# Leftover rows spread over 16 DMA engines, one first-layer pair in four through the score banks, and an order from a forward-backward scheduler, in a fused sparse attention and rational MLP kernel

## The chip, the cores and the metric

The kernel runs on one core of one Trainium2 chip. The metric is the device time of one execution in microseconds. Before the change three runs took 400.84, 405.41 and 404.82 us, median 404.82 us. One further execution was profiled: 402.03 us, with a span of 400.0 us between the first and the last thing that the profile shows.

The engines are TensorE (PE in the profile; PEld is its weight load), VectorE (DVE), ScalarE (ACT), GpSimd (POOL) and SyncE (SP). In this kernel POOL and SP do next to nothing but issue DMAs, each in the order of its own list.

## The reference

The work is an attention with two kinds of sparse mask, whose output is reshaped to 4,608 tokens of 512 features and put through two dense layers with a rational activation between them.

```python
B, H, S, D = 8, 8, 576, 64          # stride = 32
scores = (1 / sqrt(D)) * q @ k.transpose(0, 1, 3, 2)
rel = pos[:, None] - pos[None, :]
mask_local   = (rel >= 0) & (rel < stride)                      # heads 0 to 3
mask_strided = (rel >= 0) & (pos % stride equal for query, key)  # heads 4 to 7
scores = where(mask, scores, -1e9)
attn = softmax(scores)
x = (attn @ v).transpose(0, 2, 1, 3).reshape(4608, 512)
h = x @ w_in                        # 512 x 2048
P = a[0] + a[1] * h + a[2] * h**2 + a[3] * h**3
Q = 1 + |b[0]| * |h| + |b[1]| * h**2
out = (P / (Q + 1e-6)) @ w_out      # 2048 x 512
```

Inputs and outputs are float32; the kernel computes in bfloat16 with float32 sums.

## The kernel before

**Batches and chunks.** The eight batches of the attention go one after another (batch 0 to 7). The first 512 of a batch's 576 positions give four tiles of 128 tokens, which make up one chunk of 512 tokens for the dense layers (chunk 0 to 7). The 64 leftover positions of all batches make up chunk 8, the last.

**Attention of one batch.** `loads` and its helpers fetch the batch. `load_qk` brings the 512 main rows of q and k in two parts: part 0 is heads 4 to 7 (strided mask), part 1 is heads 0 to 3 (local mask), into `qn` and `kn`; part 2 brings the leftover rows into `qm` and `km`. `load_v` brings v into `VL` (local heads), `VT` (strided heads) and `VW` (leftover rows of the strided heads). All of these are issued by POOL, since they also turn float32 into bfloat16; the q, k and v of batch 0 alone come as float32 through SP and are turned by DVE, ACT and POOL. `scores` then has these steps:

- T: SP issues four DMA transposes of part 0 into `sT` (batch 0 does it on PE). `sT` has one buffer, so batch b+1's transposes wait for the last matmul of batch b that reads it.
- R2, R3: PE rearranges part 1 of k and q through PSUM into `kL` and `qL`.
- S and L: PE computes the strided and the local scores in PSUM on top of a mask that is added by matmuls; ACT takes the exponential into `ES` and `EL`.
- TL and X: SP issues two DMA transposes of the leftover rows into `LT`; PE computes the leftover rows' scores; ACT takes the exponential into `EX` and `EW`. This is the step that frees `sT`.

`attend` multiplies by v (five tiles, four main and one leftover), DVE divides by the row sums into `XR`, and SP issues a DMA transpose of each tile into `XT` (leftover tile: `XW`). Batches 0 and 1 transpose their main tiles on PE.

**Dense layers.** `dense1` is the first layer of a chunk: 16 blocks of 128 hidden features, computed two by two ("a pair", 8 matmuls of 128x512) into one of four PSUM tiles; ACT copies a pair to `HB`. Then comes the rational function: DVE takes |h| (L991 on uint16 views), b1|h|+b0 (L1003), times |h| (L1006); ACT makes 1/Q by Ln and Exp (L1015, L1018); DVE evaluates P by Horner (L1029, L1032, L1034, L1036, L1039) and multiplies with 1/Q (L1042). Chunks 2 to 7 do the DVE steps on all 16 blocks at once (8,192 elements a partition), the others in smaller groups. `dense2` is the second layer (64 matmuls of 128x512 a chunk, in groups of 8), and ACT copies its result to `OS`, from which SP writes to HBM.

**PSUM.** Four tiles of two banks each: S (scores), A (attention output), H and O. First-layer pairs alternate between H and O for chunks 0 to 2 and use H alone from chunk 3 on; the second layer uses O, and A and S for the last chunk.

**What sets the order.** Nothing in the program text does. Every operation is recorded with its engine, its dependencies, an estimated cost and a key. `Program.schedule` runs a list scheduler over them: whenever an engine is free, it takes the ready operation with the lowest key. The keys come from the table `KT` (about one number for each kind of operation and batch or chunk). The result is one fixed list for each engine, and an engine works through its list strictly in turn, waiting on semaphores at its head. Matmuls of all kinds are recorded through two helper lines, so the profile knows them as L634 (and L637 for PE transposes); they are told apart by their tiles.

Of the kernel before, what the change touches and what calls it, by code (L numbers as in the profile page):

```python
# [15 lines left out]
def _bf16_bits(x):  # L16
# [26 lines left out]
}  # L43

# [58 lines left out]
class Program:  # L103
# [32 lines left out]
    def schedule(self):  # L136
        import heapq
        for i, op in enumerate(self.ops):
            op.idx = i
            op.nwait = 0  # L140
            op.ready = 0.0
# [18 lines left out]
        while left:  # L160
# [15 lines left out]
            t, e = best  # L176
# [133 lines left out]
def bass_strided_sparse_attn__then__act_rational_pade_kernel(nc, q, k, v, moe_w_in, moe_w_out, moe_a, moe_b, out):  # L310
# [8 lines left out]
    CH = 512  # L319
# [3 lines left out]
    HL, NHO, DA, TB, NF0 = 4, 3, 0, 1, 70  # L323
# [72 lines left out]
    mz = np.where((hh_[:, None] == hh_[None, :]) & (dz >= 0) & (dz % 8 == 0), 0.0, NEG)  # L396
    rx = np.zeros((64, 192))
# [91 lines left out]
    def load_qk(b, key, part, x):  # L489
# [8 lines left out]
        else:  # L498
            add("POOL", (lambda e: e.dma_start(
                sml[i][64:128, 0:256], src[b, 4:8, 512:576, :].rearrange("h (p g) d -> h p (g d)", g=4))),  # L500
                [n_free[x][2][i], ini[id(sml[i])], hw0], 0.7, key, g, 0.25)
            for hh in range(2):
                add("POOL", (lambda e, hh=hh: e.dma_start(
# [91 lines left out]
    def loads(b):  # L595
        if b == 0:
            loads0()
            for x in (1, 0):
                load_qk(0, -955 - x, 2, x)
# [577 lines left out]
```

## Time and profile before

| | |
|---|---|
| three runs | 400.84, 405.41, 404.82 us |
| median | 404.82 us |
| profiled execution | 402.03 us |
| its span | 400.0 us |
| mean granted TensorE clock | 0.92 |
| busy: PE, DVE, ACT, POOL | 329.1, 322.8, 267.6, 171.3 us |
| DMA packets, bytes | 148,631, 41.87 MB |

Busy time of an engine is a mean over stages that are limited by different things, so the share alone decides nothing; the table by stretch and the chain of waits do. In the rows below a line number is that of the kernel before; `psS<-LT` reads "written to PSUM tile S, read from LT". In a row of the chain of waits the two numbers are start and length in us.

### The profile page before, as it was taken

To read this page: it belongs to the slowest core of one execution; us is meant where nothing else is said; L and a number is where in the kernel's file an instruction comes from. 1 tells how busy PE (TensorE), PEld (TensorE's weight loads), DVE (VectorE), ACT (ScalarE), POOL (GpSimd) and SP (SyncE) were. 2 spreads that over 40 slices of the span, in tenths; PEclk is the share of its full clock that TensorE was granted. 3 is DMA by queue.
4 is the path that set the end of the run, shared out by engine and by line. 5 is a ranking of instruction groups with operands and counts; after the bars stand their busy time and mean duration, and the time that the engine had idled before them with its cause. 6 is when DMAs were issued, how large, how long until landed. Compare 5 with 4: busy or idle time off the path is not lost.

```text
span 400.0 us, 9314 instructions
## 1 busy us (share of the span) xinstructions
PE 329.1 (82%) x4150; PEld 164.6 (41%) x4150; DVE 322.8 (81%) x276; ACT 267.6 (67%) x228; POOL 171.3 (43%) x203
## 2 busy tenths in 40 slices
PE   6686258457999769989999998999999999869930
PEld 6543225133544324444444544444444455534400
DVE  3436875965999997468998999999999899999930
ACT  2516366657498838856996799898379579686320
POOL 0999488225695489369657904900000000000000
PEclk9959759958999969999999999999999999998965
DMA  7999999999999998899999588743022222202202
GB/s 243 199 99 170 150 148 75 144 190 137 108 130 131 148 132 81 112 164 158 129 160 111 55 117 85 110 81 77 12 51 54 52 54 52 52 2 52 52 23 82
DMA packets 148631, 41.87 MB, mean 105 GB/s; under 512 B 121328, under 2 KB 143536, under 8 KB 148592
## 3 DMA queue, kind: packets, MB, share of 16 engines
q0 software_dynamic: 97376, 16.94, 52.7%
q1 hardware_dynamic: 51216, 24.34, 32.9%
q8 instruction: 32, 0.52, 0.6%
q14 instruction: 7, 0.06, 0.1%
HBM read 36.90 MB, written 9.44 MB: 116 GB/s over the span
## 4 chain that ended last, share of the span: by engine, by line
PE 36%; DVE 28%; DMA 16%; POOL 5%; SPq 5%; ACT 5%; issue 2%
PE psO L634 17%; PE psH L634 14%; DMA LT<-qm 5%; DVE UU L1006 4%; DVE T L1032 4%; DVE T L1042 3%; DVE T L1036 3%; DMA sT<-qn 3%; DVE UU L1003 3%; DVE T L991 3%; DVE T L1029 2%; PE psA L634 2%; SPq L691 2%; PE psS L634 2%; DMA XT<-XR 2%; DVE XR L885 2%
## 5 line engine op out<-in xcount | busy, mean ns | idle before, releaser
L634 PE MATMUL psO<-Wout,T 128*128 128x512 bf16 x512 | 120.8, 385 | 3.1 <-ACT OS L1106 3.1
L634 PE MATMUL psH<-XT,Win 128*128 128x512 bf16 x416 | 104.1, 394 | 9.9 <-DMA XT<-XR 6.1
L977 ACT ACTIVATE HB<-psH 128x1024 bf16<-128x1024 f32 x60 | 61.3, 1022 | 39.5 <-PE psH L634 39.2
L1015 ACT ACTIVATE UU<-UU,cst 128x2048 bf16<-128x2048 bf16 (+1 forms) x38 | 72.5, 1908 | 15.7 <-DVE UU L1006 15.6
L634 PEld LDWEIGHTS psO<-Wout,T 128*128 128x128 bf16 x512 | 48.6, 99 | 60.9 <-ACT OS L1106 4.1
L1018 ACT ACTIVATE UU<-UU 128x2048 bf16<-128x2048 bf16 (+1 forms) x38 | 69.2, 1822 | 0.6
L634 PEld LDWEIGHTS psH<-XT,Win 128*128 128x128 bf16 x416 | 39.7, 100 | 60.8 <-issue 7.0
L1042 DVE TENSOR_TENSOR T<-T,UU 128x4096 bf16<-128x4096 bf16 (+2 forms) x23 | 41.8, 1825 | 10.2 <-ACT UU L1018 9.8
L1006 DVE TENSOR_TENSOR UU<-UU,T 128x4096 bf16<-128x4096 bf16 (+2 forms) x23 | 41.6, 1825 | 0.5
L1032 DVE TENSOR_TENSOR T<-T,HB 128x8192 bf16<-128x8192 bf16 (+3 forms) x17 | 41.1, 2417 | 0.5
L1036 DVE TENSOR_TENSOR T<-T,HB 128x8192 bf16<-128x8192 bf16 (+3 forms) x17 | 41.0, 2414 | 0.4
L536 POOL DMA_DIRECT2D VT<-in_v_dram x48 | 37.9, 818 | 0.0
L524 POOL DMA_DIRECT2D VL<-in_v_dram x24 | 22.1, 937 | 27.2 <-PE psA L634 27.2
L991 DVE TENSOR_SCALAR T<-HB 128x8192 uint16<-128x8192 uint16 (+3 forms) x17 | 23.4, 1378 | 12.4 <-ACT HB L977 12.4
L1003 DVE TENSOR_SCALAR UU<-T,coef 128x4096 bf16<-128x4096 bf16 (+2 forms) x23 | 25.5, 1121 | 0.6
L634 PE MATMUL psO<-XT,Win 128*128 128x512 bf16 x96 | 24.4, 399 | 0.0
L1029 DVE TENSOR_SCALAR T<-HB,coef 128x8192 bf16<-128x8192 bf16 (+3 forms) x17 | 24.0, 1413 | 0.4
L885 DVE TENSOR_TENSOR XR<-psA,RC 128x512 bf16<-128x512 f32 (+1 forms) x35 | 22.1, 630 | 2.8 <-DMA XT<-XR 1.6
L1039 DVE TENSOR_SCALAR T<-T,coef 128x8192 bf16<-128x8192 bf16 (+3 forms) x17 | 23.6, 1386 | 0.4
L1034 DVE TENSOR_SCALAR T<-T,coef 128x8192 bf16<-128x8192 bf16 (+3 forms) x17 | 23.5, 1380 | 0.4
L1106 ACT ACTIVATE OS<-psO 128x1024 f32<-128x1024 f32 x16 | 16.4, 1022 | 9.2 <-PE psO L634 9.1
L544 POOL DMA_DIRECT2D VW<-in_v_dram x28 | 22.5, 813 | 0.0
(151 smaller groups left out, 383.6 us busy)
## 6 DMA issues: line engine op xcount, KB each, us to landing
out_dram<-OS SPq DMA_DIRECT2D x72, 128.0 KB
kn<-in_k_dram POOLq DMA_DIRECT2D x14, 256.0 KB, 5.9
qn<-in_q_dram POOLq DMA_DIRECT2D x14, 256.0 KB, 6.9
Win<-in_moe_w_in_dram POOLq DMA_DIRECT2D x4, 512.0 KB, 9.6
Wout<-in_moe_w_out_dram POOLq DMA_DIRECT2D x1, 2048.0 KB, 18.8
VL<-in_v_dram POOLq DMA_DIRECT2D x24, 72.0 KB, 4.4
VT<-in_v_dram POOLq DMA_DIRECT2D x48, 32.0 KB, 3.3
HB<-in_k_dram SPq DMA_DIRECT2D x2, 512.0 KB, 5.1
```

Of the source, the lines that this page charges most:

```text
L536: add("POOL", (lambda e, h=h, c=c: e.dma_start(VT[i][64 * c:64 * c + 64, h, :, 0:64], v[b, 4 + h, 0:512, :].rearrange("(x c g) d -> c x g ...
L634: return lambda e: e.matmul(out_ap, l, r, start=start, stop=stop, skip_group_check=True)
L977: o2 = add("ACT", (lambda a, hb=hb, ps=ps, f=f: a.activation(hb[:, f:f + 2, :], ps[:, :, :], AF.Copy)), [o1, old], ca(1024), key.of("HB"))
L991: d1 = add("DVE", (lambda d, hb=hb, t3=t3, g_=g_: d.tensor_scalar(t3.bitcast(dt.uint16)[:, g_, :], hb.bitcast(dt.uint16)[:, g_, :], 0x7FFF ...
L1003: d2 = add("DVE", (lambda d, u=u, t3=t3, sl=sl, HG=HG: d.tensor_scalar(u[:, 0:HG, :], t3[:, sl, :], b1_ap, b0_ap, op0=Alu.mult, op1=Alu.add)),
L1006: d3 = add("DVE", (lambda d, u=u, t3=t3, sl=sl, HG=HG: d.tensor_tensor(u[:, 0:HG, :], u[:, 0:HG, :], t3[:, sl, :], op=Alu.mult)), [d2], ct ...
L1015: ln = add("ACT", (lambda a, u=u, zl=zl: a.activation(u[:, zl, :], u[:, zl, :], AF.Ln, bias=cst[:, 0:1], scale=1.0)), [d3, cons], 0.28 + w ...
L1018: ex.append(add("ACT", (lambda a, u=u, zl=zl: a.activation(u[:, zl, :], u[:, zl, :], AF.Exp, scale=-1.0)), [ln], 0.21 + w * 0.000833, kz + ...
L1029: d4.append(add("DVE", (lambda d, hb=hb, t3=t3, h0=h0, h1=f0 + gn: d.tensor_scalar(t3[:, h0:h1, :], hb[:, h0:h1, :], a_ap[3], a_ap[2], op0 ...
L1032: d5 = add("DVE", (lambda d, hb=hb, t3=t3, g_=g_: d.tensor_tensor(t3[:, g_, :], t3[:, g_, :], hb[:, g_, :], op=Alu.mult)), [d4], ctt(n), k ...
L1036: d7 = add("DVE", (lambda d, hb=hb, t3=t3, g_=g_: d.tensor_tensor(t3[:, g_, :], t3[:, g_, :], hb[:, g_, :], op=Alu.mult)), [d6], ctt(n), k ...
L1042: d9 = add("DVE", (lambda d, t3=t3, u=u, sl=sl, HG=HG: d.tensor_tensor(t3[:, sl, :], t3[:, sl, :], u[:, 0:HG, :], op=Alu.mult)), [d8, ex], ...
```

## The change

1. **Leftover rows.** The DRAM side of the leftover loads is written with the 16 groups of rows as the outer dimension instead of the heads: `qm` and `km` rows of the strided heads, and `VW`. For the local heads two DMAs, of two heads each, become four, of one head each. The leftover rows of the strided heads thus stand in `qm`/`km` in another order, and the mask columns and the slices that read `LT` are permuted to match. 32 more DMAs are issued by POOL over the run.
2. **PSUM tiles.** From chunk 3 on, every fourth first-layer pair goes to S instead of H (`PM1 = "HHHS"`). A tile is chosen by name tables (`PM1`, `PM2`, `PAV`, `PSC`).
3. **A piece of the polynomial.** `DA` goes from 0 to 1: in chunks 2 to 7 the first Horner step a3·h+a2 is done by ACT for 8 of the 16 blocks (one instruction on 4,096 elements), by DVE for the other 8.
4. **Order.** `KT` has other numbers, and above all every operation's key is replaced by its place in a fixed list `PRIORITY` of 1,230 entries, which a forward-backward scheduler has made. `loads` no longer has a special order for batch 1, all four loads of `Win` are recorded together, and the load of `Wout` is recorded behind the loads of batch 2. In `dense2` the groups of one PSUM tile now depend on each other, so that no list can turn them round.

```diff
+PRIORITY = [
+    6, 49, 160, 166, 162, 191, 51, 9, 8, 76, 108, 20, 21, 107, 186, 179, 188, 18, 22, 73, 33, 34, 68, 48,
...
+    1222, 1228, 1226, 1225, 1229
+]
...
         for i, op in enumerate(self.ops):
             op.idx = i
+            if PRIORITY:
+                op.key = PRIORITY[i]
...
-    HL, NHO, DA, TB, NF0 = 4, 3, 0, 1, 70
+    HL, DA, TB, NF0 = 4, 1, 1, 70
+    PM1, PM2, PAV, PSC = "HHHS", "O", "A", "S"
...
+    mz = mz[:, 16 * (ar % 4) + ar // 4]
...
             add("POOL", (lambda e: e.dma_start(
-                sml[i][64:128, 0:256], src[b, 4:8, 512:576, :].rearrange("h (p g) d -> h p (g d)", g=4))),
+                sml[i][64:128, 0:256], src[b, 4:8, 512:576, :].rearrange("h (p g) d -> p h (g d)", g=4))),
...
-            for hh in range(2):
-                add("POOL", (lambda e, hh=hh: e.dma_start(
-                    sml[i][0:32, :].rearrange("x (g y d) -> x y g d", g=4, y=2)[:, hh],
-                    src[b, hh:4:2, 512:576, :].rearrange("a (p g) d -> a p g d", g=4))),
-                    [n_free[x][2][i], ini[id(sml[i])], hw0], 0.7, key + 0.01, g, 0.15)
+            for h in range(4):
+                add("POOL", (lambda e, h=h: e.dma_start(
+                    sml[i][16 * (h // 2):16 * (h // 2) + 16, :].rearrange("x (g y d) -> x y g d", g=4, y=2)[:, h % 2],
+                    src[b, h, 512:576, :].rearrange("(p g) d -> p g d", g=4))),
+                    [n_free[x][2][i], ini[id(sml[i])], hw0], 0.65, key + 0.01, g, 0.15)
...
-                        v[b, 4:8, 512:576, :].rearrange("h (i g) d -> g h i d", g=4)[2 * gp + j])),
+                        v[b, 4:8, 512:576, :].rearrange("h (i g) d -> g i h d", g=4)[2 * gp + j])),
...
-                                             LT[64 * j:64 * j + 64, 0, gh, 64 + 16 * h:80 + 16 * h], False, False))
+                                             LT[64 * j:64 * j + 64, 0, gh, 64 + h:128:4], False, False))
...
-                pn = "HO"[npair[0] % 2] if c < NHO else "H"
+                pm = "HO" if c < 3 else PM1
+                pn = pm[npair[0] % len(pm)]
...
-                    last = add("PE", makers, [[res[kk][2] for kk in range(q0, q0 + 4)], g2.ops, p_free[pn]],
+                    last = add("PE", makers, [[res[kk][2] for kk in range(q0, q0 + 4)], g2.ops, p_free[pn], last],
```

The change moves nearly every instruction. Three places show what the next part speaks of; an `x2` at a row's end means two such instructions in a row.

The first is POOL's list around the load of `Wout` (the second layer's weights). Before, from the leftover rows of batch 2 on (L499, L503, `VW`) to the main rows of batch 3 (`kn`, `qn`):

```order
L499 DMA km<-in_k_dram 64x1x256
L499 DMA qm<-in_q_dram 64x1x256
L503 DMA km<-in_k_dram 32x4x64 x2
L503 DMA qm<-in_q_dram 32x4x64 x2
L536 DMA VT<-in_v_dram 64x4x64
L544 DMA VW<-in_v_dram 64x1x64 x4
L486 DMA Wout<-in_moe_w_out_dram 128x16x512
L495 DMA kn<-in_k_dram 128x4x256
L495 DMA qn<-in_q_dram 128x4x256
```

After, from the same leftover rows on (L575, L579 are the lines that were L499, L503; L571 was L495, L562 was L486, L620 was L544):

```order
L579 DMA qm<-in_q_dram 16x4x64 x2
L575 DMA km<-in_k_dram 64x1x256
L571 DMA qn<-in_q_dram 128x4x256
L579 DMA qm<-in_q_dram 16x4x64
L579 DMA km<-in_k_dram 16x4x64
L571 DMA kn<-in_k_dram 128x4x256
L562 DMA Wout<-in_moe_w_out_dram 128x16x512
L620 DMA VW<-in_v_dram 64x1x64
L571 DMA kn<-in_k_dram 128x4x256
```

`Wout` has moved behind the first q and k loads of batch 3, which can only be issued once batch 2's transposes into `sT` have read `qn` and `kn`. Two of the leftover loads of batch 2 now stand behind such a q load too.

The second place is PE's list from the scores of batch 2 to its leftover scores (the rows with `LT`). Before, from the mask and the strided scores (`psS<-sT`) on:

```order
L634 MATMUL psS<-IDN,MK 64x512 x4
L634 MATMUL psS<-sT 64x64 x32
L634 MATMUL psS<-IDN,MK 64x512 x4
L634 MATMUL psS<-qL,kL 64x32 x64
L634 MATMUL psA<-VL,EL 32x65 x16
L634 MATMUL psA<-VT,ES 32x65 x16
L634 MATMUL psH<-XT,Win 128x512 x8
L634 MATMUL psS<-MK 64x192 x4
L634 MATMUL psS<-IDN,MK 64x64 x4
L634 MATMUL psS<-LT,kL 64x32 x8
```

After, the end of the same stretch; five pairs (`XT,Win`) and all four main tiles of the attention (`VL,EL` with `VT,ES`) stand between the local scores and the leftover scores, of which these are the last three pairs and two tiles (L700 was L634):

```order
L700 MATMUL psH<-XT,Win 128x512 x8
L700 MATMUL psA<-VL,EL 32x65 x16
L700 MATMUL psA<-VT,ES 32x65 x16
L700 MATMUL psO<-XT,Win 128x512 x8
L700 MATMUL psA<-VL,EL 32x65 x16
L700 MATMUL psA<-VT,ES 32x65 x16
L700 MATMUL psH<-XT,Win 128x512 x8
L700 MATMUL psS<-MK 64x192 x4
L700 MATMUL psS<-IDN,MK 64x64 x4
L700 MATMUL psS<-LT,kL 64x32 x8
```

So the leftover scores, which wait for the transposes into `LT`, stand several microseconds of matmuls later in the list, behind work that does not need them.

The third place is PE's list where the first pairs of chunk 3 begin (`psH<-XT,Win`), among the second layer of chunk 0 (`psO<-Wout,T`) and the scores of batch 4. Before:

```order
L634 MATMUL psO<-Wout,T 128x512 x8
L637 MATMUL psS<-IDN,qn 64x128 x16
L634 MATMUL psH<-XT,Win 128x512 x8
L634 MATMUL psO<-Wout,T 128x512 x8
L634 MATMUL psS<-IDN,MK 64x512 x4
L634 MATMUL psS<-sT 64x64 x32
L634 MATMUL psH<-XT,Win 128x512 x8
L634 MATMUL psO<-Wout,T 128x512 x8
```

After:

```order
L700 MATMUL psO<-Wout,T 128x512 x16
L700 MATMUL psH<-XT,Win 128x512 x8
L700 MATMUL psS<-MK 64x192 x4
L700 MATMUL psS<-IDN,MK 64x64 x4
L700 MATMUL psS<-LT,kL 64x32 x8
L700 MATMUL psS<-LT,sT 64x16 x32
L700 MATMUL psS<-LT 64x64 x4
L700 MATMUL psO<-Wout,T 128x512 x8
L700 MATMUL psH<-XT,Win 128x512 x8
L700 MATMUL psS<-XT,Win 128x512 x8
```

Before, four groups of chunk 0's second layer stand ahead of chunk 3's first pair; now all eight do. From the first to the last pair of chunk 3 seven second-layer groups stood in between, now four. The last row is a pair in PSUM tile S.

At the start SP's list has changed as well: the float32 q of heads 0 to 3 goes first, then v, then the constants and the rest of q and k. POOL's first loads (`Win`) wait for the q load of heads 0 to 3, which was the fourth of SP's loads and is now the first. At the end the last four pairs of chunk 8 have four second-layer groups between them each.

More of the change, by code (lines that the diff above doesn't have):

```diff
@@ L591, in loads0 @@
         t3_free[1] = [evl, v_ev[1, 0]]
-        load_win(0, -990)
-        load_win(1, -989)
+        for z in range(NW1):
+            load_win(z, Key("LW", z))
     def loads(b):
@@ L681, in scores @@
                 key = Key("X", b, n)
-            pn = sets.get(name, "S")
+            pn = sets.get(name, "S") if first else PSC[nsc[0] % len(PSC)]
+            nsc[0] += name not in ("T", "TL")
             ps = PS[pn]
@@ L1074, in dense2 @@
         tail = c == NCH - 1
-        used = ["A", "S"] if tail else ["O", "O"]
+        used = ["A", "S"] if tail else [PM2[(2 * c + z) % len(PM2)] for z in range(2)]
         if tail:
@@ L1083, in dense2 @@
                             makers.append(mm(ps[:, e_, :], gl(res[kk], 2 * i2 + e_), Wout[:, kk, :], kk == 0, kk == NF - 1))
[L1084 removed]
+                    o = add("PE", makers, [[res[kk][2] for kk in range(q0, q0 + 2)], g2.ops, p_free[used[i2]], done[-2:]],
+                            4 * 0.216, base + q0 + 0.1 * i2)
                     done.append(o)
@@ L1089, in dense2 @@
             if not tail:
+                last = []
                 for q0 in range(0, NF, 4):
```

35 lines of the change are left out of this document (12 added, 23 removed), and 104 rows, old and new, of tables (KT, PRIORITY).

## The prediction

> **What bounds the kernel now.** I read the page first, then a table of busy time by stretch, then the chain of work that ended last, then the waits. The page's head and three of its rows of 40 slices of 10 us:
>
> ```profile
> span 400.0 us, 9314 instructions
> PE 329.1 (82%) x4150; PEld 164.6 (41%) x4150; DVE 322.8 (81%) x276; ACT 267.6 (67%) x228; POOL 171.3 (43%) x203
> PE   6686258457999769989999998999999999869930
> DVE  3436875965999997468998999999999899999930
> PEclk9959759958999969999999999999999999998965
> ```
>
> PE and DVE are both four fifths busy, and each has its gaps mostly in the first 18 slices. There the granted clock falls to 0.5 as well. The table by stretch puts numbers to that (columns: length, busy us of PE, PEld, DVE, ACT, POOL, clock, DMA share, GB/s):
>
> ```profile
> 75.00:100.00 25.00, 12.92 (x276) 6.28 (x276) 16.13 (x17) 16.72 (x15) 8.19 (x10) 0.73 1.37 166
> 100.00:135.00 35.00, 33.75 (x558) 16.77 (x559) 34.24 (x35) 27.59 (x25) 25.66 (x29) 1.00 1.22 125
> 135.00:150.00 15.00, 8.86 (x78) 3.60 (x77) 14.79 (x9) 6.88 (x7) 9.52 (x10) 0.77 1.28 142
> 150.00:180.00 30.00, 28.56 (x428) 13.69 (x430) 18.20 (x16) 22.77 (x22) 20.25 (x25) 1.00 1.13 119
> 180.00:250.00 70.00, 67.21 (x1107) 33.04 (x1104) 65.52 (x44) 58.46 (x54) 43.44 (x49) 1.00 1.03 116
> 250.00:310.00 60.00, 59.97 (x434) 27.00 (x433) 59.12 (x33) 48.33 (x35) 9.15 (x10) 1.00 0.35 64
> 310.00:340.00 30.00, 30.00 (x156) 15.12 (x155) 28.17 (x12) 23.11 (x18) 0.00 (x0) 1.00 0.23 53
> 340.00:385.00 45.00, 38.57 (x184) 17.96 (x181) 41.53 (x40) 27.13 (x20) 0.00 (x0) 0.95 0.15 35
> ```
>
> Between 75 and 100 us PE and DVE both idle and the clock is 0.73: 8.9 us of DVE are lost. Between 135 and 180 PE idles first, at clock 0.77, and DVE afterwards: 12.0 us of DVE are lost, 11.8 of them after 150. From 180 to 340 PE misses 2.8 us of 160 and DVE 7.2; ACT misses 30.1. After 340 it is DVE. The chain says why (start, length, what):
>
> ```profile
> 19.10 5.51 DMA qm<-in_q_dram
> 77.57 14.23 DMA LT<-qm
> 135.15 8.12 DMA XT<-XR
> 143.31 3.59 PE psH L634 x8
> 308.68 1.73 PE psH L634 x8
> 312.17 1.02 ACT OS L1106
> 315.03 2.29 DVE T L1042
> 381.96 0.70 DVE T L1042
> ```
>
> The early losses are DMAs: the leftover rows at 19, the transposes of batch 2's leftover rows, 14.2 us on their way, and the transposes of chunk 3's input, 8.1 us. Through the middle the chain is PE at 1.73 us a group of 8 matmuls, from 313 on ACT and DVE.
>
> **The leftover loads.** What they cost, from the DMA view (size, median us to landing) and the groups (count, busy, mean ns):
>
> ```profile
> qm<-in_q_dram POOLq DMA_DIRECT2D x16, 16.0 KB, 4.8
> km<-in_k_dram POOLq DMA_DIRECT2D x16, 16.0 KB, 5.5
> VT<-in_v_dram POOLq DMA_DIRECT2D x48, 32.0 KB, 3.3
> L503 POOL DMA_DIRECT2D km<-in_k_dram x16 | 18.6, 1167 | 0.1
> L499 POOL DMA_DIRECT2D qm<-in_q_dram x8 | 5.2, 653 | 0.0
> ```
>
> The nearest row for a small load with 64 partitions outside on both sides is `VT`, twice as large and 2.2 us faster than `km`. So batch 0's leftover rows, which are on the chain, gain up to 2.2 us. Against that POOL issues four DMAs of 64 rows for two of 128: a row of that size takes 0.65 us (L499), so 4 x 0.65 - 2 x 1.17 = 0.3 us more for `km`, and about as much for `qm`, under 1 us for a batch. I take -1 us, ends -2.2 and +1. The Trainium skill ("DMA: Bandwidth & Descriptors", rules for kernel authors) says that the outermost dimension caps the engines a DMA uses, which gives the same sign. Another rule on that page speaks against this edit: join small transfers, since under 64 KB a DMA is mostly overhead. By it the two extra DMAs would cost and nothing would land sooner: +1 instead of -1. I keep the `VT` row as the nearer evidence; no run here separates the two yet. The permuted mask and the strided slices of `LT` change no count; I put them at nothing.
>
> **`Wout` and batch 2.** Two rows of the lists of POOL and SP, one of the DMA view, and four of the waits (total, times, longest):
>
> ```profile
> 71.04 1.18 POOL L486 DMA_DIRECT2D Wout<-in_moe_w_out_dram  x1
> 70.39 2.92 SPq L691 DMA_TRANSPOSE sT<-qn  x2
> Wout<-in_moe_w_out_dram POOLq DMA_DIRECT2D x1, 2048.0 KB, 18.8
> PE psS L634 <- DMA sT<-qn: 7.3, 1, 7.3
> PE psH L634 <- ACT HB L977: 4.0, 7, 1.2
> PE psH L634 <- DMA XT<-XR: 6.1, 1, 6.1
> ACT HB L977 <- PE psH L634: 39.2, 28, 7.3
> ```
>
> `Wout` is issued while batch 2's transposes into `sT` are under way, and takes 18.8 us. PE then waits 7.3 us for those transposes, and later for `LT`. In the new list `Wout` stands behind q and k loads that need these transposes finished, so it can't slow them. It now meets the transposes into `LT` and `XT` of batch 2, but PE's list has five pairs (5 x 1.73 = 8.7 us) and four attention tiles before the leftover scores where it had one of each. What is late next is therefore `XT` of batch 2, with those five pairs as its cover too. I take -7.3 us for this stretch; it cannot give more than the 8.9 us that DVE loses there, nor less than 0. One new wait: POOL's q load of batch 3 waits for `sT`, and behind it are the last two leftover loads of batch 2, then SP's `LT` transposes, then the leftover scores. If the pairs don't cover that, part of the 7.3 comes back.
>
> **Chunk 3.** PE's first pair of chunk 3 waits for `XT` until 143.3 and then runs at half pace: 3.59 us against 1.73. In the new list eight second-layer groups stand ahead of it instead of four: 4 x 1.73 = 6.9 us later, about the 6.1 us that PE waits there for `XT`, so the pair starts where it did, without the wait and warm (-1.9). Four instead of seven groups stand between its pairs: -3 x 1.73 = -5.2 us to the last one, which lets DVE's 16-block steps begin. Together about -7; since the first layer of other chunks moves as well, I take -6, ends 0 and -11.8 (all that DVE loses after 150).
>
> **The Horner step on ACT.** By shape:
>
> ```profile
> L1029 DVE TENSOR_SCALAR T<-HB,coef 128x8192 bf16<-128x8192 bf16 x6 | 14.5, 2422 | 0.2
> L1029 DVE TENSOR_SCALAR T<-HB,coef 128x4096 bf16<-128x4096 bf16 x3 | 4.0, 1342 | 0.1
> L1015 ACT ACTIVATE UU<-UU,cst 128x2048 bf16<-128x2048 bf16 x34 | 67.9, 1997 | 7.7 <-DVE UU L1006 7.7
> ```
>
> DVE saves 6 x (2.42 - 1.34) = 6.5 us. Only where DVE is the later engine does that shorten anything: for certain in chunk 7 (1.1 us), at most everywhere. I take half, 3.5 us. ACT has no such instruction now; L1015 takes 2.0 us for 2,048 elements, so 4,096 take between 2.0 and 4.0, and I take 3.9, near the upper end: 23.4 us more on ACT. Its cover is ACT's idle time, 30.1 us from 180 to 340, where five of the six fall (19.5 us): 0 for now, but ACT would be 93% busy there.
>
> **Pairs in S; the rest of the order.** PE waits 4.0 us for the copy out of H in the whole run: the fourth pair in S can save at most that and must share S with the scores. I take 0, ends 0 and -4. The dependencies in `dense2` are between PE's own instructions and cost nothing. At the start q of heads 0 to 3 goes first, and `Win` follows its landing:
>
> ```profile
> 10.16 1.69 POOL L481 DMA_DIRECT2D Win<-in_moe_w_in_dram  x2 [9.71 <-DMA HB<-in_q_dram]
> 7.14 6.43 DMA T<-in_v_dram
> 13.60 1.91 ACT L644 ACTIVATE VL<-T 32x2048 bf16<-32x2048 f32 x1 [0.89 <-DMA T<-in_v_dram]
> HB<-in_k_dram SPq DMA_DIRECT2D x2, 512.0 KB, 5.1
> ```
>
> Of the four loads of q and k the last lands at 10.2 us, each some 5 to 6 us after its issue, so three of them share the last 4 us or so. With `Win` beside them instead of after them these may take twice as long: +4. v would land sooner, and ACT's turning of v (1.9 us), which now stands between its landing and the exponentials, would be done before the scores come: -2. I take 0.
>
> **Sum.** -1 - 7.3 - 6 - 3.5 = -17.8 on the profiled 402.0: 384.2 us. That execution lies 2.8 us under the median of the three runs, but above their lowest, so I put 1.4 on top: 386 us.
>
> **Rivals.** (a) *The collision only moves.* `Wout` keeps DMA busy for 18.8 us wherever it is; it now meets the transposes of `LT`, `XT` and then `sT` of batch 3, and chunk 3 starts no earlier because more stands before it. For it: DMA share above 1 in every stretch shown up to 250 us. Against it: PE's list has work ahead of the late steps. Only -3.5 and -1 are left: 402.0 - 4.5 + 1.4 = 399 us. (b) *ACT becomes the bound, and it is slower.* ACT works its list in turn; a 3.9 us instruction stands ahead of the copies that free H, and PE and DVE wait for these. ACT waits 39.2 us for PE in the whole run, so its idle time is not free to be filled at will. If the 30.1 us of idle time between 180 and 340 stay and five such instructions (19.5 us) come on top, with -7.3 and -1 from the early part: 402.0 + 19.5 - 8.3 + 1.4 = 415 us. It decides from the point where ACT's idle time in that stretch does not fall below 30 - 19.5 = 11 us. (c) *All bounds on the good side:* -2.2 - 8.9 - 11.8 - 6.5 - 4 - 2 = -35.4, so 368 us.
>
> **How the numbers follow.** The forecast has 0.57, (a) 0.20, (b) 0.11, (c) 0.12. The range reaches from 370 us, 2 us short of all bounds at once, to 403 us, which is (a) with the +4 of the start, and leaves (b) out. A difference of 2% is what runs of this kernel tell from none (they spread over 1.1%): faster than 396.7 us by the forecast and (c) together, 0.69; within 2% for (a), 0.20; slower than 412.9 us for (b), 0.11.
>
> **What would show it.** Right: PE's wait for `sT<-qn` near 80 us gone, no 14 us step for `LT` in the chain, DVE busy for more than 16.1 of the 25 us from 75 to 100; chunk 3's first pair at 1.73 us; landing of `km` near 3.3 us; DVE about 316 us busy in total, ACT about 291; no new wait of PE for HB beyond some 4 us. Wrong: an `XT` or `LT` transpose of over 10 us with PE idle behind it anywhere before 180 us, or ACT over 95% busy from 180 to 340 with PE waiting on its copies.

## The result, and the profile after

The changed kernel takes 392.5 us (median of four runs, 391.4 to 393.6); the kernel before takes 404.5 us (median of four, 400.8 to 405.4). The ratio is 0.972, with a 95% interval of 0.9654 to 0.9786: faster by 2.8%. I had forecast 386 us, with a range of 370 to 403 us.

| | before | after |
|---|---|---|
| median of the runs | 404.5 us | 392.5 us |
| profiled execution, its span | 402.0, 400.0 us | 393.6, 391.5 us |
| busy: PE, DVE | 329.1, 322.8 us | 321.6, 315.3 us |
| busy: ACT, POOL | 267.6, 171.3 us | 286.8, 169.5 us |
| DMA packets | 148,631 | 111,255 |

The page of the changed kernel, three of its rows of 40 slices (9.8 us each):

```profile
span 391.5 us, 9332 instructions
PE 321.6 (82%) x4119; PEld 164.5 (42%) x4150; DVE 315.3 (81%) x276; ACT 286.8 (73%) x234; POOL 169.5 (43%) x235
PE   0858976973799839989999999989999999997930
DVE  2433995975879895687999999999999999999930
PEclk9966996995799987998999999999999999999995
```

The holes of the first 18 slices are still there. The table by stretch, in the columns of the prediction (length, busy us of PE, PEld, DVE, ACT, POOL, clock, DMA share, GB/s):

```profile
75.00:100.00 25.00, 13.25 (x235) 6.88 (x233) 18.20 (x22) 17.71 (x16) 10.61 (x16) 0.80 1.32 165
100.00:135.00 35.00, 32.67 (x515) 16.31 (x520) 29.33 (x29) 28.20 (x25) 25.13 (x33) 0.95 0.96 104
135.00:150.00 15.00, 8.75 (x134) 3.84 (x132) 14.76 (x10) 5.99 (x5) 13.53 (x19) 0.82 1.72 168
150.00:180.00 30.00, 27.62 (x444) 14.02 (x448) 17.80 (x16) 25.14 (x22) 15.24 (x24) 0.92 1.13 138
180.00:250.00 70.00, 67.59 (x896) 32.90 (x905) 68.86 (x47) 63.74 (x52) 41.65 (x50) 1.00 0.82 110
250.00:310.00 60.00, 58.27 (x538) 27.12 (x542) 58.75 (x33) 56.25 (x41) 7.48 (x12) 1.00 0.33 58
310.00:340.00 30.00, 28.94 (x157) 15.31 (x158) 29.65 (x14) 29.46 (x20) 0.00 (x0) 1.00 0.23 53
```

Compare with the rows before. From 75 to 100 us DVE does 18.2 us of work instead of 16.1. From 100 to 180 it does 61.9 us instead of 67.2. Up to 180 us it is idle for 3.9 us more than before (its work before 75 us is 43.3 instead of 43.8 us), so nothing is won by then. From 180 to 340 it is idle for 2.7 of 160 us instead of 7.2. And DVE has 7.5 us less to do in the whole run (315.3 against 322.8), while the span is 8.5 us shorter: DVE's idle time in all hardly moved (76.2 us against 77.2). ACT is busy for 149.5 of the 160 us from 180 to 340, 93%.

The chain of waits shows where the early time went (start, length, what):

```profile
10.75 11.28 DMA coef<-in_moe_a_dram
34.31 3.59 PE psO L700 x8
79.97 12.59 DMA XT<-XR
93.37 7.06 DMA XT<-XR
100.48 3.37 PE psO L700 x8
136.88 9.72 DMA XT<-XR
146.65 3.61 PE psH L700 x8
```

The three `PE ... x8` rows are the first pairs of chunks 0, 2 and 3. Ahead of the second stand two `XT` transposes of batch 2 that take 12.6 and 7.1 us; ahead of the third, one of 9.7 us. Six rows of the waits (total, times, longest) say who stands still:

```profile
PE psO L700 <- DMA XT<-XR: 5.3, 1, 5.3
DVE XR L953 <- DMA XT<-XR: 6.3, 1, 6.3
PE psH L700 <- DMA XT<-XR: 6.8, 2, 6.1
POOL qm L579 <- DMA LT<-km: 12.1, 1, 12.1
ACT HB L1045 <- PE psH L700: 13.3, 18, 1.8
PE psH L700 <- ACT HB L1045: 1.1, 3, 0.5
```

PE's wait for `sT` of batch 2 (7.3 us before) is gone, but PE now waits 5.3 us for chunk 2's `XT` (the first row). Between the two slow transposes stands DVE: it waits 6.3 us for the first one, which reads `XR`, before it can write the last main tile of batch 2 into the same buffer, so that the second one is issued only at 93.4 us. The 6.1 us wait for chunk 3's `XT` is what it was, and POOL waits 12.1 us for a transpose into `LT`. ACT's waits for PE's pairs in H fell from 39.2 to 13.3 us; part of that idle time now holds the six new instructions.

At the start the two kernels differ like this: DVE's instructions around the copy into `sT` after the change, then PE's first pair before and after it.

```profile
20.42 0.69 DVE L711 CAST VT<-T 128x1024 bf16<-128x1024 f32 x1 [6.39 <-DMA T<-in_v_dram]
22.05 0.16 DVE L510 SCALAR_TENSOR_TENSOR coef<-coef 128x2 f32<-128x2 f32 x1 [0.94 <-DMA coef<-in_moe_a_dram]
22.13 1.22 DVE L711 COPY sT<-psS 128x2048 bf16<-128x2048 bf16 x1
```

```profile
25.47 3.39 PE L634 MATMUL psH<-XT,Win 128*128 128x512 bf16 x8 [0.69 <-ACT XT L644]
```

```profile
34.31 3.59 PE L700 MATMUL psO<-XT,Win 128*128 128x512 bf16 x8 [0.52 <-DVE XT L711]
```

The new list has two small operations that wait for late DMAs, on v and on the coefficients, ahead of the copy into `sT`, for which PE waits 4.4 us. And SP issues the second half of q at 6.8 us instead of 2.8, behind the loads of v and the identity, so that ACT turns it at 15.95 us instead of 9.87. The first pair comes 8.8 us later.

So two questions are open. Which part of the change made the 12 us? And what were the early stalls worth, since some moved, some stayed, and one was added?

### The profile page after: what moved, and what is told of

Same layout as the page of the kernel before. It is cut to its first block, busy times and chain, and to the rows that moved or that the text cites. A ratio compares the mean times of both kernels' runs of the same rounds, so it can differ in the third digit from the quotient of the medians.

```text
span 391.5 us, 9332 instructions
## 1 busy us (share of the span) xinstructions
PE 321.6 (82%) x4119; PEld 164.5 (42%) x4150; DVE 315.3 (81%) x276; ACT 286.8 (73%) x234; POOL 169.5 (43%) x235
## 2 busy tenths in 40 slices
DMA packets 111255, 41.72 MB, mean 107 GB/s; under 512 B 83952, under 2 KB 106160, under 8 KB 111216
## 4 chain that ended last, share of the span: by engine, by line
DVE 37%; PE 25%; DMA 19%; POOL 5%; SPq 5%; issue 4%; ACT 2%; POOLq 0%; DVEq 0%
PE psO L700 9%; DMA XT<-XR 9%; PE psH L700 8%; DVE T L1104 6%; DVE UU L1074 5%; DVE T L1100 5%; DVE T L1110 5%; PE psS L700 3%; PE psA L700 3%; DVE T L1107 3%; DVE T L1102 3%; DMA coef<-in_moe_a_dram 3%; DVE UU L1071 3%; POOL VT L612 3%; POOL VL L600 2%
## 5 line engine op out<-in xcount | busy, mean ns | idle before, releaser
L700 PE MATMUL psO<-Wout,T 128*128 128x512 bf16 x482 | 111.4, 379 | 4.4 <-issue 2.4
L700 PE MATMUL psH<-XT,Win 128*128 128x512 bf16 x336 | 82.8, 389 | 7.9 <-DMA XT<-XR 6.8
L700 PEld LDWEIGHTS psO<-Wout,T 128*128 128x128 bf16 x512 | 48.4, 98 | 57.3 <-ACT OS L1176 1.4
L1045 ACT ACTIVATE HB<-psH 128x1024 bf16<-128x1024 f32 x48 | 49.1, 1024 | 13.4 <-PE psH L700 13.3
L700 PEld LDWEIGHTS psH<-XT,Win 128*128 128x128 bf16 x336 | 31.5, 98 | 47.5 <-DMA XT<-XR 7.4
L600 POOL DMA_DIRECT2D VL<-in_v_dram x24 | 25.6, 1074 | 28.4 <-PE psA L700 28.1
L612 POOL DMA_DIRECT2D VT<-in_v_dram x48 | 35.9, 778 | 2.4 <-PE psA L700 1.8
L700 PE MATMUL psO<-XT,Win 128*128 128x512 bf16 x96 | 25.9, 417 | 5.8 <-DMA XT<-XR 5.3
L579 POOL DMA_DIRECT2D qm<-in_q_dram x32 | 20.4, 643 | 12.1 <-DMA LT<-km 12.1
L1093 ACT ACTIVATE T<-HB,coef 128x4096 bf16<-128x4096 bf16 x6 | 22.8, 3799 | 0.9 <-DVE UU L1074 0.9
L951 DVE RECIPROCAL RC<-psA 128x8 f32<-128x8 f32 (+1 forms) x35 | 6.9, 197 | 19.0 <-PE psA L700 18.8
## 6 DMA issues: line engine op xcount, KB each, us to landing
Wout<-in_moe_w_out_dram POOLq DMA_DIRECT2D x1, 2048.0 KB, 18.9
```

The source lines that it names most:

```text
L612: add("POOL", (lambda e, h=h, c=c: e.dma_start(VT[i][64 * c:64 * c + 64, h, :, 0:64], v[b, 4 + h, 0:512, :].rearrange("(x c g) d -> c x g ...
L700: return lambda e: e.matmul(out_ap, l, r, start=start, stop=stop, skip_group_check=True)
L1045: o2 = add("ACT", (lambda a, hb=hb, ps=ps, f=f: a.activation(hb[:, f:f + 2, :], ps[:, :, :], AF.Copy)), [o1, old], ca(1024), key.of("HB"))
```

## Experiments: the parts against the order

My theory after the two traces: DVE's smaller work is the gain, the early stalls cancel out. The rivals: the loads, or the order itself. Each kernel was timed beside the kernel before on the same chip (405.05 us there, median of 17, for the first four). A ratio is that of a kernel's time to the time of the kernel before, with its 95% interval in brackets.

**The table of order numbers taken away.**

```
 PRIORITY = [
-    6, 49, 160, 166, 162, 191, 51, 9, 8, ...
 ]
```

> The changed kernel, but its table of order numbers is empty, so that the list scheduler goes by the formula keys that stand beside it; loads, the Horner step on ScalarE and the fourth pair in S stay. DVE was busy 7.5 us less after the change (315.3 against 322.8) while the span fell by 8.5 us. If the smaller work of DVE is the whole gain, this kernel has that work too and takes 392 to 396 us. If the order carries the gain, or is needed to make room for ScalarE's larger share, it takes 401 us or more, with the difference in idle time of DVE.

Measured: 418.4 us (413.8 to 420.2), ratio 1.032 (1.0267 to 1.0375). All the other parts are in it, DVE's smaller work too (314.9 us), and it is slower than the kernel before. So the smaller work is not the whole gain. Two waits show where the formula keys lose: in the execution profiled (420.2 us) DVE waits 19.2 us for ACT's half of the Horner step, and PE 20.8 us for transposes into `sT`. The keys beside the table were another start than those before, so this doesn't price the order against the old one; that takes the parts put singly into the old kernel.

**Only the leftover loads, in the old kernel.**

```
-  sml[i][64:128, 0:256], src[b, 4:8, 512:576, :].rearrange("h (p g) d -> h p (g d)", g=4)
+  sml[i][64:128, 0:256], src[b, 4:8, 512:576, :].rearrange("h (p g) d -> p h (g d)", g=4)
-  for hh in range(2):   # 32 rows each
+  for h in (0, 2, 1, 3):   # 16 rows each
...
-  v[b, 4:8, 512:576, :].rearrange("h (i g) d -> g h i d", g=4)[2 * gp + j]
+  v[b, 4:8, 512:576, :].rearrange("h (i g) d -> g i h d", g=4)[2 * gp + j]
...
```

> The kernel before, in its own order, with only the leftover loads in their new form (and the mask and slices that go with them). If the DVE's work decides, the time stays within 1% of 404.4 us: my own term was -1 us. If the 37,000 packets that disappear were what made the early transposes late, the wait for sT of batch 2 (7.3 us) and the wait for XT of chunk 3 (6.1 us) shrink by more than half and the time falls to about 395 us.

Measured: median 404.4 us of twelve runs (395.1 to 406.8), beside 405.05. The means differ by 1.4 us with a standard error of 1.0, so no difference shows that is clear of the noise. The two fastest took 395.1 and 400.9 us; by these two alone the ratio would be 0.983 (0.9765 to 0.9903), so a gain of 1 to 2% in some executions isn't excluded. Its page has 111,255 packets, as the changed kernel's: 37,376 fewer, a quarter of all. The waits that were to shrink did not: in the execution profiled (406.0 us) PE waits 11.5 us for `sT` of batch 2, where it was 7.3, and 6.3 us for `XT` of chunk 3, where it was 6.1. Of the reshaped loads only `VW` has a time to landing on the page, and it lands no sooner: 2.8 us here, 2.9 before. The Trainium skill ("DMA: Bandwidth & Descriptors", rules for kernel authors) asks for an outermost dimension that lets a DMA use all 16 engines. Here it did no harm, and no run shows a gain in time from it that is clear of the noise.

**Only the Horner step, in the old kernel.**

```
-    HL, NHO, DA, TB, NF0 = 4, 3, 0, 1, 70
+    HL, NHO, DA, TB, NF0 = 4, 3, 1, 1, 70
```

> The kernel before with only the first half of the Horner step moved to ScalarE for the six chunks that run in blocks of 16; the list scheduler places the six new instructions by the keys of before, and moves some neighbours. If DVE's work decides, 6 x (2.42 - 1.34) = 6.5 us go: 398 us. By the half that I forecast: 401 us. If the new order is needed to make room on ScalarE, the time stays at 404 us or grows, with PE or DVE waiting for ScalarE's copies.

Measured: 475.6 us (473.8 to 480.1), ratio 1.179 (1.1728 to 1.1849). None of the numbers had this size. The waits, and one of the six places from the timeline:

```profile
DVE T L1032 <- ACT T L1025: 41.0, 6, 19.9
PE psH L634 <- ACT HB L977: 41.6, 16, 18.6
```

```profile
232.78 1.91 ACT L1018 ACTIVATE UU<-UU 128x2048 bf16<-128x2048 bf16 x1
235.71 3.77 ACT L1025 ACTIVATE T<-HB,coef 128x4096 bf16<-128x4096 bf16 x1
```

```profile
239.52 4.42 DVE L1032 TENSOR_TENSOR T<-T,HB 128x8192 bf16<-128x8192 bf16 x1 [3.15 <-ACT T L1025]
```

By the old keys ACT does its half of the step (L1025) only behind the Ln and Exp passes (L1015, L1018). Its key comes from a row of `KT` (`D4`) that was never used while `DA` was 0, so this run prices one bad place for the step; whether the old order has a good one wasn't tried. DVE waits for ACT's half in all six chunks, up to 19.9 us, and while the two are behind, the copies that free H are late, for which PE waits 41.6 us. DVE's work fell to 316.9 us and the time grew by 70 us. In the changed kernel the list of waits has no row in which DVE waits for this instruction (there L1093).

**The Horner step back on DVE, in the new order.** ACT does 1 block of 16 instead of 8; the planner's costs are left, so that the lists stay.

```
-  t3[:, f0:f0 + 8, :], hb[:, f0:f0 + 8, :], AF.Identity, bias=a_ap[2], scale=a_ap[3])),
+  t3[:, f0:f0 + 1, :], hb[:, f0:f0 + 1, :], AF.Identity, bias=a_ap[2], scale=a_ap[3])),
...
-  h0 = f0 + (8 if gn == 16 and DA else 0)
+  h0 = f0 + (1 if gn == 16 and DA else 0)   # for DVE's part
```

> The changed kernel in its own order, but ScalarE does one block of 16 in the Horner step instead of 8, and DVE the other 15. DVE gets about 6 x 0.93 = 5.6 us back and ScalarE loses some 19 us of work. If DVE's work decides: 392.5 + 5.6 = 398 us. By half of it: 395 us. If ScalarE at 93% had become the bound in the second half, the time falls below 392 us instead.

Measured: 394.7 us (393.0 to 396.9), ratio 0.9764 (0.9724 to 0.9803).

```profile
L1097 DVE TENSOR_SCALAR T<-HB,coef 128x7680 bf16<-128x7680 bf16 x6 | 13.7, 2278 | 0.2
```

The changed kernel has 0.972 in its first runs and 0.9667 in those below, so the step is worth 0.4 to 1.0%, 1.8 to 3.9 us (the first pair of intervals overlaps, the second doesn't). On DVE it saves 5.0 us: with the three instructions on 8 blocks that both kernels have, 17.7 us here against 12.7 (nine on 4,096 elements, 1,414 ns each) in the changed kernel. It is a small part of the 12 us, and ACT is not the bound: with 16 us less work on it (271.0 against 286.8) nothing gets faster. From 180 to 340 us ACT is idle for 25.3 us here and for 10.5 with the step, so the step was paid out of idle time. My theory falls here. Order, loads and pairs in S are worth some 10 us together without this step.

**All pairs of chunks 3 and later in H, in the changed kernel.**

```
-    PM1, PM2, PAV, PSC = "HHHS", "O", "A", "S"
+    PM1, PM2, PAV, PSC = "H", "O", "A", "S"
```

> The changed kernel with every pair of the first layer from chunk 3 on in H, none in S; the table of order numbers stays, and the list scheduler moves some neighbours because other copies now free the banks. I put the fourth pair in S at 0, ends 0 and -4: so 392 to 396 us here. If the bank in S is what lets PE run ahead of ScalarE in the second half, where ScalarE is 93% busy, PE's wait for the copies out of H grows from a few us to 10 or more and the time goes above 397 us.

Measured: 418.8 us (417.8 to 419.3), ratio 1.0345 (1.0301 to 1.0389), beside 405.3 for the kernel before. Its waits and two of its stretches:

```profile
PE psH L700 <- ACT HB L1045: 18.7, 13, 4.3
```

```profile
180.00:250.00 70.00, 64.23 (x816) 30.60 (x804) 59.12 (x41) 55.33 (x43) 33.96 (x46) 0.98 0.91 105
250.00:310.00 60.00, 53.21 (x568) 24.01 (x558) 51.59 (x35) 48.67 (x38) 11.85 (x16) 1.00 0.36 58
```

PE waits 18.7 us for the copies out of H, where the changed kernel has 1.1 us; DVE does 16.9 us less in these two stretches. The scheduler also moved some neighbours, so the 26 us are not the bank's alone. But the wait that grew is the one that a second tile can take away: while ACT's copy out of H is late, PE can go on in S.

## Experiments: the early stalls

In the diffs from here on, `put` moves operations within the finished list of one engine; everything else keeps its place. These four ran on one chip with the kernel before (405.1 us, median of 11). The first is the measure for the others.

> The changed kernel as it is, as the measure for the three that stand beside it: 392.5 us, within 0.5%.

Measured: 391.6 us (388.9 to 393.2), ratio 0.9667 (0.9626 to 0.9708).

**The old start.** Behind the scheduler the first operations of four lists are put into the order before.

```
     pr.schedule()
+    put("SP", [c_idn, k0, q0, k1, q1, c_mk, v x6, cst, coef_a, coef_b], at the front)
+    put("ACT", [qn, qn, kL, VL], at the front)
+    put("DVE", [kn, kn, sT, qL, VL, VT, coef], behind the memsets)
+    put("PE", [R1, R2, R3], behind 41 fillers)
```

> The changed kernel with the first operations of SP, ScalarE, DVE and PE in the order of the kernel before (identity first, then the four q and k loads, the masks, v; on DVE the copy into sT ahead of the v casts and of the operation on coef); Win then waits for the last of the four loads, as it did. The first first-layer pair should go from 34.3 back to about 25.5 us. If a late start counts in full, the time falls by 9 us to 384 us. If the stretch from 30 to 50 us is bound by the loads of batch 1 in both kernels (the scores of batch 1 start at 48.7 us after the change and at 49.0 before it, whatever the start), the time stays within 2 us of 392.5.

Measured: 390.6 us (388.1 to 393.2), ratio 0.9661 (0.9623 to 0.9699): no difference that can be told. PE's first pair, and one of its waits:

```profile
27.68 2.99 PE L700 MATMUL psO<-XT,Win 128*128 128x512 bf16 x8 [0.52 <-DVE XT L711]
```

```profile
PE psA L700 <- DMA sT<-kn: 5.5, 1, 5.5
```

The first pair comes 6.6 us sooner, and PE then waits 5.5 us for batch 1's transposes into `sT`. In the changed kernel that wait is not there, since PE arrives later. So the late start costs nothing that shows: what follows it waits for the transfers of batch 1 either way.

**`Wout` later.**

```
     pr.schedule()
+    put("POOL", [Wout], behind the first two q and k loads of batch 4)   # 72 us -> 96 us
```

> The changed kernel with the load of Wout moved on POOL's queue from 72 us to behind the two q and k loads of about 103 us; the order of all else stays. Its 18.9 us then lie behind the transposes into LT and XT of batch 2 (12.6 us each in the chain now) and ahead of the first second-layer group at 119.6 us, with a few us to spare at most. If Wout is what makes those transposes late, they land in 5 to 7 us, the first pair of chunk 2 goes from 100.5 to about 94 us, and DVE is busy for more than 20 of the 25 us from 75 to 100 (18.2 now). If that stretch decides the end, the time falls to 387 us; if the transposes of chunk 3 decide again at 146 us, it stays within 2 us of 392.5. A time above 395 us means that Wout now lands too late.

Measured: 385.0 us (383.5 to 386.9), ratio 0.9517 (0.9481 to 0.9553): 6.6 us under the changed kernel, all six runs below its lowest. Three stretches, and from the timeline of PE the first pairs of chunks 2 and 3:

```profile
75.00:100.00 25.00, 20.62 (x326) 10.10 (x325) 23.95 (x29) 22.80 (x22) 10.09 (x15) 1.00 0.97 111
100.00:135.00 35.00, 26.79 (x481) 12.89 (x483) 23.36 (x23) 22.80 (x20) 21.38 (x31) 0.90 1.37 164
150.00:180.00 30.00, 26.83 (x450) 13.32 (x449) 24.83 (x20) 23.51 (x20) 22.37 (x29) 1.00 1.19 132
```

```profile
90.38 1.90 PE L700 MATMUL psO<-XT,Win 128*128 128x512 bf16 x8 [1.49 <-DMA XT<-XR]
140.46 1.89 PE L700 MATMUL psH<-XT,Win 128*128 128x512 bf16 x8
```

One piece of its chain, and two rows of its waits:

```profile
86.00 4.34 DMA XT<-XR
```

```profile
PE psO L700 <- DMA Wout<-in_moe_w_out_dram: 4.1, 1, 4.1
PE psA L700 <- DMA VL<-VL: 5.8, 2, 4.0
```

The `XT` transposes of batch 2 land after 3.3 to 4.3 us where they took 7.1 to 12.6, chunk 2 starts at 90.4 instead of 100.5 us, DVE does 24.0 instead of 18.2 us from 75 to 100, and the clock is 1.00 instead of 0.80. Then `Wout` and the loads behind it cost some of that again between 100 and 135 (PE waits 4.1 us for it, DVE does 6.0 us less). Chunk 3 starts at 140.5 us without any wait for `XT`. Only `Wout` was moved, so `Wout` is what made batch 2's transposes late. The Trainium skill ("DMA: Bandwidth & Descriptors", section "Issuing engines are not separate DMA queues") says that DMAs of all issuing engines run on the same 16 DMA engines and interleave. Here that is up to 12.6 against at most 4.3 us for the same four transposes, with and without a 2 MB load from POOL beside them.

**The q and k loads of batch 5 behind the v loads of batch 4.**

```
     pr.schedule()
+    put("POOL", [kn, qn, kn, qn of batch 5], behind VT of batch 4)   # 132 us -> 146 us
```

> The changed kernel with the four q and k loads of batch 5 (2 MB, issued from 131.6 to 134.6 us) behind the v loads of batch 4 on POOL's queue instead of ahead of them; all else stays. They lie just ahead of the last transposes into XT of chunk 3, for which PE waits 6.1 us until 146.65. If these loads are what makes the transposes late, PE's first pair of chunk 3 starts at 141 to 143 us, the gap of DVE from 152.0 to 160.4 us closes by about 4 us, and the time falls to about 388 us. If the transposes are late whatever is loaded beside them (the v loads of batch 4 now start 3 us sooner in their place), nothing changes: 392.5 us within 2.

Measured: 396.6 us (394.9 to 398.8), ratio 0.9796 (0.9759 to 0.9834): 5.0 us slower than the changed kernel. PE's first pair of chunk 3, two waits between 140 and 182 us, and the stretch after:

```profile
141.76 1.90 PE L700 MATMUL psH<-XT,Win 128*128 128x512 bf16 x8 [0.85 <-DMA XT<-XR]
```

```profile
PE psA L700 <- DMA VL<-VL: 9.3, 1, 9.3
DVE RC L951 <- PE psA L700: 13.4, 4, 10.6
```

```profile
150.00:180.00 30.00, 19.69 (x275) 9.12 (x272) 16.99 (x13) 16.82 (x16) 16.68 (x27) 0.83 1.10 127
```

The first half came out as forecast: with these loads out of the way the pair starts at 141.8 us instead of 146.7. But SP's list has the transposes into `sT` of batch 5 ahead of the copies within `VL` of batch 4, and the transposes now wait for the later loads. SP works its list in turn, so the first copy within `VL` is issued at 158.8 us instead of 156.2, while PE now comes 4.9 us sooner: PE waits 9.3 us for it, and DVE 10.6 us for PE. The stall of chunk 3 is a collision that can be moved, and moving it alone made a longer one.

## Experiments: the same move in the old order

The last four ran on one chip (the kernel before: 405.3 us, median of 21). Two of them ask what my step on `Wout` is worth by itself; the run with all pairs in H, above, was the third.

```
     pr.schedule()
+    put("POOL", [Wout], behind the first two q and k loads of batch 3)   # 71 us -> 76 us
```

> The kernel before, with one line of POOL's list moved: Wout behind the first two q and k loads of batch 3, so that it can't be issued until batch 2's transposes into sT have landed. This is the step that I priced at -7.3 us, alone. By that price: 397 us, with PE's 7.3 us wait for sT gone and no new one. If the collision only moves, the transposes into LT and XT of batch 2 (14.2 us and over 10 us) stay as late as they are or grow, the first pair of chunk 2 stays near 100 us, and the time stays within 2 us of 405.

Measured: 401.9 us (400.1 to 406.4), ratio 0.9934 (0.9897 to 0.9971). From its chain of waits and its waits:

```profile
78.22 11.38 DMA LT<-qm
```

```profile
PE psH L634 <- DMA XT<-XR: 2.0, 1, 2.0
```

PE's wait for `sT` near 80 us is gone, and 0.3 to 1.0% is won by it (2.7 us by the ratio). The transposes into `LT` still take 11.4 us, and a wait of 2.0 us for `XT` of chunk 2 is new; the wait for chunk 3's `XT` is 3.9 us where it was 6.1. This is between my price and the rival, nearer to the rival. It is POOL's half of the step only: the five pairs that were to cover the next transfer stand in the new list of PE, not in this one.

```
     pr.schedule()
+    put("POOL", [Wout], behind all q and k loads of batch 3)   # 71 us -> 93 us
```

> The kernel before, with Wout behind all q and k loads of batch 3, the leftover ones too, so at 85 to 98 us instead of 71; its 18.9 us end before the first second-layer group, which stands at 128.2 us now. If Wout's neighbours in time are what matters, the transposes into sT, LT and XT of batch 2 are all quick, DVE loses 4 to 7 us less between 75 and 100 us, and the time is 395 to 398 us, in the old order with none of the rest of the change. If the stall of chunk 3 at 143 us or the engines' own order in the second half decides, it stays within 2 us of 405.

Measured: 409.5 us (405.7 to 412.2), ratio 1.0106 (1.0068 to 1.0144): slower by about 1%. Two stretches, and PE's first pair of chunk 2:

```profile
75.00:100.00 25.00, 17.33 (x373) 8.49 (x372) 23.10 (x26) 19.55 (x18) 13.57 (x15) 0.86 0.90 110
100.00:135.00 35.00, 25.45 (x407) 12.38 (x406) 23.98 (x23) 21.62 (x21) 18.84 (x24) 0.90 1.53 152
```

```profile
106.99 3.57 PE L634 MATMUL psH<-XT,Win 128*128 128x512 bf16 x8 [6.56 <-DMA XT<-XR]
```

DVE wins 7.0 us from 75 to 100 (23.1 against 16.1) and loses 10.3 from 100 to 135 (24.0 against 34.2). The same move to about the same time gave -6.6 us in the new order and +4.2 us here. In the new order what is lost from 100 to 135 is 6.0 us, and the time comes back from 150 to 180 (24.8 instead of 17.8 us of DVE). One difference stands in the traces. In the new order SP has issued all four `XT` transposes of batch 2 by 86.0 us, and they have landed when `Wout` follows at 95.8. In the old order the last of them is issued at 95.8 us, behind `Wout` at 93.2, and takes 11.1 us; PE waits 6.6 us for it (the row above), a wait that the kernel before doesn't have. How much of the loss is due to this wasn't tried.

**`Wout` in quarters, with the old start, in the new order.**

```
-  Wout[:, :, :], one DMA, one semaphore
+  Wout[:, 4 * z:4 * z + 4, :] for z in 0..3, a semaphore each
...
-  [..., g2.ops, ...]
+  [..., g2[q0 // 4].ops, ...]
     pr.schedule()
+    put("POOL", [quarter 0, quarter 1], behind the first two q and k loads of batch 4)
+    put("POOL", [quarter 2, quarter 3], behind VT of batch 3)
```

> The changed kernel with the old start (as in the run with the old start) and Wout loaded in four quarters, each with a semaphore of its own: two where the run with the late Wout has the whole (95 us), two behind the v loads of batch 3; a second-layer group waits for its quarter alone. With Wout late as a whole, PE waited 4.1 us for it at 123 us and the v loads of batch 3 took 12.8 us behind it. If those two waits cost time, the time falls from 385 to 380 to 383 us. If the second half, where DVE is over 97% busy, has the slack to take up what is won before 125 us, or v lands as late behind the quarters, it stays at 385 us within 1.5.

Measured: 386.4 us (382.8 to 389.2), ratio 0.9526 (0.9472 to 0.9579): as with the whole of `Wout`.

```profile
PE psA L713 <- DMA VL<-VL: 6.1, 2, 5.3
```

PE no longer waits for `Wout`, but it waits as long for `VL` of the batches around (6.1 us; with the whole of `Wout` 5.8). (Both totals are up to 180 us.) Of the two waits one went, and nothing came of it. The lowest time seen is thus that of the changed kernel with `Wout` later, 385.0 us, with this one level with it.

## Why the prediction was right, and where its terms were wrong

The sign and the range held, and the gain is clear of the noise; the forecast was 6.5 us too low. The measured time lies as far from my 386 us as from rival (a)'s 399, so the time alone does not choose between them, and the sum did not hold term by term. One of the signs of being wrong that I had named came as well: an `XT` transpose of over 10 us before 180 us with PE idle behind it.

- **The leftover loads, -1 us (ends -2.2 and +1).** The size held: -0.6 us between the medians, within the error of nothing. The reason for a gain, a sooner landing on the chain, was not seen: `VW` lands no sooner, and in the changed kernel DVE's copy into `sT` was what the start waited for.
- **`Wout` and batch 2, -7.3 us.** This is the step that failed most. PE's wait for `sT` went, as said. What was to be late next, `XT` of batch 2 with five pairs as cover, was later than the cover: the pairs end at about 87 us, the transposes took 12.6 and 7.1 us, and the first pair of chunk 2 stands until 100.5 us. DVE's idle time, from which the term's bound was drawn, fell by 2.1 us from 75 to 100 (8.9 to 6.8) and grew by 4.9 from 100 to 135 (0.8 to 5.7). POOL's half alone gave 2.7 us in the old order. The collision that is left costs 6.6 us, which is what the run with the late `Wout` wins back. Rival (a), that the collision only moves, was right on this point though not on the sum.
- **Chunk 3, -6 us.** Nothing of it shows in DVE's idle time: from 150 to 180 us DVE is idle for 12.2 us, where it was 11.8. The eight second-layer groups were to move PE past the wait. But `XT` came later too (the transpose that PE waits for was issued at 136.9 us and took 9.7), so that the pair starts at 146.7 instead of 143.3 us, still waits 6.1 us and still runs at half pace (3.6 us). I moved PE's side of the wait and left the DMA's side where it was. The other half of the term held: with four second-layer groups in between instead of seven, the last pair of chunk 3 starts at 174.5 us, 3.5 us sooner than before (178.0).
- **The Horner step, -3.5 us.** Right in size: 1.8 to 3.9 us, with 5.8 us less for DVE in this step (18.5 to 12.7) where I had 6.5. Its cover held: ACT's idle time from 180 to 340 us took it up (25.3 us without the step, 10.5 with it). The 93% came as forecast (129.9 + 19.5 = 149.4 of 160 us; measured 149.5), and the instruction takes 3.8 us where I had 3.9.
- **Pairs in S, 0 (ends 0 and -4).** The bound was drawn from PE's 4.0 us of waiting for H in the old kernel, where ACT had 30 us to spare. In the new order ACT has 10.5, and without the pairs in S (and with the neighbours that the scheduler moved) PE waits 18.7 us and the time is 26 us longer. The bound of a wait that hardly exists before says nothing when another edit makes its releaser busier.
- **The start, 0 (ends -2 and +4).** The first pair came 8.8 us later, more than the +4: the later issue of the second half of q on SP's list and the two waiting operations ahead of the `sT` copy on DVE's had been left out of the sum. In the time of the whole it came to 1.0 us between the medians, which is within the noise, so the 0 held for another reason than mine: the transfers of batch 1 are late either way.
- **Rival (b), ACT as the bound.** It did not come in the new order, where ACT's idle time from 180 to 340 fell to 10.5 us, below the 11 us that I had named. It is what happened with the old keys, at 475.6 us.

So the forecast was right partly by luck. Of two terms of -13.3 us together DVE's idle time up to 180 us shows nothing: it grew by 3.9 us. What made up for it was DVE's idle time from 180 to 340 us, which fell by 4.5 us in an order that I had priced at nothing, and DVE's work, smaller by 7.5 us (5.8 of them the Horner step). With 0.4 us less idle time after 340 that makes +3.9 - 4.5 - 7.5 - 0.4 = -8.5 us, the difference of the profiled spans. This is a count and not a cause: when the Horner step goes back to DVE, no more than 3.9 us come back. How much of the 10 us that remain without the step is the order's in the second half, and how much is a better place of the early work, is only argued from the two tables by stretch; no run took the old order for one half and the new for the other.

## What to carry to other kernels

Price the parts of a change that comes with a new order together: the half of a Horner step on ScalarE was worth -1.8 to -3.9 us where the list puts it ahead of the need, and +70 us under the old keys, which put it behind the Ln and Exp passes of its own chunk. When a large load is moved out of one transfer's way, look at the transfers that run at its new time and at who waits for them; here every load that was moved had a next victim, and the same move of one load won 6.6 us in one order and lost 4.2 in the other. And check what is late next on both sides of a wait, the engine's and the DMA's, since moving only the engine moves the wait along with it.

## What the runs showed of the hardware

A quarter fewer DMA packets (111,255 instead of 148,631, with the same bytes but for 0.15 MB) changed the mean time by 1.4 us with a standard error of 1.0, though the DMA share is above 1 in most stretches up to 180 us. A DMA over 16 partitions costs POOL about half of one over 32 (0.53 us against 1.17 for `km`, 0.64 against 1.06 for `qm`), so that 64 such DMAs take 37.2 us of POOL in the changed kernel and the 32 before took 35.4:

```profile
L579 POOL DMA_DIRECT2D km<-in_k_dram x32 | 16.8, 529 | 6.0 <-DMA LT<-qm 5.7 <-issue 0.3
```

The four DMA transposes of batch 2 into `XT` landed after 7.1 to 12.6 us with the 2 MB load of `Wout` beside them or just before them, and after 3.3 to 4.3 us without it; the load took 18.9 us itself.
